# Stores of made left sides and pair outputs on GpSimd's queue, in an attention block followed by two wide layers

## The chip, the core and the metric

One core of a Trainium2 chip runs the whole program. Its engines work side by side, each through its own list of instructions in order: PE (TensorE, matrix products), ACT (ScalarE), DVE (VectorE), POOL (GpSimd) and SP (SyncE, which here only issues transfers between the device's memory, DRAM, and the core's memory, SBUF). A transfer (DMA) is issued by an engine's queue and then runs on the core's 16 DMA engines. The metric is the device time of one execution in microseconds (us); smaller is better.

## What is computed

An attention over pooled keys and values, then two layers with two matrix products each, on 4608 rows of 512 numbers, all in fp32 (the products' operands are split into a high and a low part, so each product is three matmuls).

```python
B, H, S, D = q.shape                      # 8, 8, 576, 64
k_p = k.reshape(B, H, S // 8, 8, D).mean(axis=3)   # and v_p the same
attn = softmax(q @ k_p.T / sqrt(D))
x = (attn @ v_p) rearranged to (B * S, H * D)      # 4608 x 512
h = x @ w_in                                       # 512 x 2048
x = maximum(0.01 * h, h) @ w_out                   # 2048 x 512
h = x @ w2_in
return (h * clip(h + 3, 0, 6) / 6) @ w2_out
```

## The kernel before

The kernel first writes down its whole work as a list of tasks, each with its engine, a cost, its inputs and its outputs, and a planner then simulates the engines on these costs and emits each engine's instructions in the order that it found. A transfer is a task of an engine called "dma" in that list, whatever queue issues it (on_dma, L294). Semaphores are put in from what each instruction reads and writes. Transfers of one queue take eight semaphores in turn, so a transfer also waits for the one eight before it on its queue to land.

The rows are cut in tiles of 512. The first three tiles go through the first layer as plain products (moe_tile), the rest in pairs of tiles (Pair1, in three pairs), and the second layer in five pairs of 920 or 924 columns (Pair). In a pair, a product of 2 x 2 blocks is computed with seven products (PRODUCTS, L863) of sums of blocks. Each of the seven needs a left side, a combination of weight blocks that is the same for every pair. Left sides are made once, while other products run, and kept in DRAM: first_weights (L925), pair_weights (L943) and second_weights (L975) load raw weights, decode them, combine quarters (combine, L911) and call split_off (L890). split_off takes one of three staging buffers called st, lets ACT cast the high part into it and DVE subtract to get the low part, and then issues two stores of 256 KB from it to DRAM (L906): one into the array for a pair's first product, one into that for its second. In second_weights the raw words come by a load of 1 MB (L982, raw<-wq), and ACT (L622, L624) and DVE (L627, L635) decode them.

A pair then streams left sides back from DRAM (stream, L1044; the load is L1049) into buffers that PE reads, in first (L1113) for its first product and second (L1219) for its second. second ends four times with a copy or sum of the result into an st buffer and a store of it (L1275): into x2 in DRAM for Pair1, into the output for Pair. Pairs also prepare the next pair's right sides from x2 (loads L1067).

All of these transfers, loads and stores alike, are issued by SP (DMA, that is nc.sync) in the planner's order. SP works strictly in order: a store whose data DVE has not yet made holds back the loads behind it, and a load whose buffer PE still reads holds back the stores behind it. GpSimd (GP, that is nc.gpsimd) only clears some buffers in the first 96 us.

Of the kernel before, what the change touches and what calls it, by code (L numbers as in the profile page):

```python
# [247 lines left out]
def attention_moe_moe(ctx: ExitStack, tc: tile.TileContext, qt, kt, vm, vr, wt, wq, eye, mask, out):  # L248
# [14 lines left out]
    PE, ACT, DVE, GP, DMA = nc.tensor, nc.scalar, nc.vector, nc.gpsimd, nc.sync  # L263
# [6 lines left out]
    def f32(ap):  # L270
        return ap.bitcast(F32)
# [22 lines left out]
    def on_dma(nbytes, emit, reads, writes):  # L294
        add("dma", nbytes / 340 + 60, emit, reads, writes)
# [4 lines left out]
    def copy(dst, src, n, psum=False, scale=None, extra=0):  # L300

        if scale is None:
            a = lambda: ACT.copy(out=dst.ap(), in_=src.ap())  # L303
            b = lambda: DVE.tensor_copy(out=dst.ap(), in_=src.ap())
        else:
            a = lambda: ACT.mul(out=dst.ap(), in_=src.ap(), mul=scale)  # L306
            b = lambda: DVE.tensor_scalar_mul(dst.ap(), src.ap(), scale)
        add("act", act_cost(n, psum) + extra, a, [src], [dst], other("dve", dve_cost(n, not psum), b))

    def subtract(dst, a, b, n):  # L310
        on_dve(
            n,
            lambda: DVE.tensor_tensor(out=dst.ap(), in0=a.ap(), in1=f32(b.ap()), op=ALU.subtract),  # L313
            [a, b],
            [dst],
        )
# [65 lines left out]
    def part(v, key, cut):  # L382
        return View(v.buf, (*v.key, key), lambda t: cut(v.cut(t) if v.cut else t))
# [503 lines left out]
    def new_st(dtype=F32):  # L887
        return buf("st", [128, 2, 512], dtype, 3)

    def split_off(left, f, v, s):  # L890

        st = new_st(F32R)
        src = View(v.buf, v.key, lambda t: v.cut(t).rearrange("p (g n) -> p g n", g=2))
        hi, lo = [st(i, lambda t, i=i: t[:, :, 256 * i : 256 * i + 256]) for i in range(2)]
        copy(hi, src, 512)
        subtract(lo, src, hi, 512)
        for g, (dst, cut) in enumerate(
            [
                (left.first[f // 2], lambda t: t[:, s, f % 2, :]),
                (left.second[s][f // 4], lambda t: t[:, f % 4, :]),  # L900
            ]
        ):
            dst = dst((s, f), cut)
            on_dma(
                262144,
                lambda dst=dst, g=g: DMA.dma_start(out=f32(dst.ap()), in_=f32(st.get()[:, g, :])),  # L906
                [st()],
                [dst],
            )

    def combine(left, f, q):  # L911
        (q11, q12), (q21, q22) = q
        plus(q22, q21, q22, 512)
        split_off(left, f, q22, 4)
        minus(q21, q11, q21, 512)
        split_off(left, f, q21, 3)
        minus(q11, q22, q11, 512)
        split_off(left, f, q11, 2)
        minus(q12, q12, q11, 512)
        split_off(left, f, q12, 6)  # L920
# [102 lines left out]
    class Pair:  # L1023
# [195 lines left out]
        def second(self, last=False):  # L1219

            n = self.n
            x, z, w = [[self.bank(k) for _ in range(2)] for k in "xzw"]
            y = {}
            for s in range(PRODUCTS):
# [3 lines left out]
                for f in range(8):  # L1228
# [10 lines left out]
                    b = [[self.slot(f, i, j) for j in range(2)] for i in range(2)]  # L1239
# [28 lines left out]
                if done:  # L1268
                    c, i, j = done
                    dst = self.place_of(i, j)  # L1270
                    for a, b in ((0, 1), (1, 2)) if last and s == 6 else ((0, 2),):
                        to, writes = dst(a, b)
                        on_dma(
                            256 * n * 2 * (b - a),
                            lambda c=c, a=a, b=b, to=to: DMA.dma_start(out=to(), in_=y[c].get()[:, a:b, 0:n]),  # L1275
                            [part(c, r) for r in range(a, b)],
                            writes,
                        )
# [82 lines left out]
    for u in units[: C["n32"]]:  # L1361
        g = u.g
        a = a13 if g else a12
# [254 lines left out]
```

## Time and profile before

| | us |
|---|---|
| three runs | 1597.93, 1599.67, 1600.58 |
| their median | 1599.67 |
| the profiled execution | 1599.98 |
| its span, first to last instruction | 1598.2 |
| PE busy in it | 1579.4 |
| DVE, ACT, GpSimd busy | 1187.1, 999.8, 2.3 |
| granted TensorE clock, mean | 0.997 |

The profiled execution is one run of the program, recorded by the chip. Busy time counts an engine's instructions; on PE the ends of matmuls are modelled. Rows of the timeline give start, duration, engine, line of the kernel, operation, what is written and read (names without buffer numbers), how many instructions were merged, and in brackets the idle time of the engine before it with what ended it. SPq rows are issues of transfers. Rows of waits give who waited for whom: total us, times, longest. A row of the table of stretches gives the stretch, its length, the busy time of PE, of PE's weight loads, of DVE, ACT and GpSimd with the count of instructions, then the granted TensorE clock as a share of full speed (2.4 GHz), the mean busy share of the 16 DMA engines, and GB/s. A tile's view gives duration in ns as least, median and most.

### The profile page before, as it was taken

How to read it: one execution, taken by the hardware profiler on the slowest of the kernel's cores; microseconds unless marked ns; L12 is line 12 of the kernel's file. 1: busy time of each engine (PE TensorE's matmuls, PEld its weight loads, DVE VectorE, ACT ScalarE, POOL GpSimd, SP SyncE). 2: the span in 40 equal slices, each digit the busy share in tenths (PEclk: the TensorE clock that was granted, in tenths of full speed). 3: DMA queues.
4: the chain of work that ended last, by engine and by line, in shares of the span. 5: the costliest groups of instructions: out<-in, count | busy, mean ns of one | idle time of the engine just before them, and what ended most of it. 6: DMA issues, size and time to landing. Idle time of an engine off the chain costs nothing.

```text
span 1598.2 us, 23912 instructions
## 1 busy us (share of the span) xinstructions
PE 1579.4 (99%) x8285; PEld 1350.3 (84%) x8285; DVE 1187.1 (74%) x2150; ACT 999.8 (63%) x2469; POOL 2.3 (0%) x12
## 2 busy tenths in 40 slices
PE   9999999999999999999989999999999999999999
PEld 8888887788788887878878888888888888888888
DVE  7989778677979776885687569658755955885494
ACT  6978577677977577666655455546545645654454
POOL 0000000000000000000000000000000000000000
PEclk9999999999999999999999999999999999999999
DMA  8988687668896898779988657856775686676564
GB/s 293 326 310 291 229 271 247 226 209 274 278 322 201 283 314 300 235 241 320 336 288 293 214 208 249 274 209 222 256 236 206 228 281 211 224 247 224 210 237 151
DMA packets 129480, 406.39 MB, mean 254 GB/s; under 512 B 18640, under 2 KB 47440, under 8 KB 107600
## 3 DMA queue, kind: packets, MB, share of 16 engines
q1 hardware_dynamic: 129360, 404.87, 74.3%
q8 instruction: 66, 1.08, 0.3%
q14 instruction: 54, 0.44, 0.1%
HBM read 317.79 MB, written 87.03 MB: 253 GB/s over the span
## 4 chain that ended last, share of the span: by engine, by line
PE 86%; DVE 6%; DMA 4%; ACT 2%; issue 1%; SPq 0%; ACTq 0%; DVEq 0%
PE y L1012 35%; PE h L1012 21%; PE a L1012 12%; PE y L757 2%; PE y L759 2%; PE y L758 2%; PE h L708 2%; PE h L710 2%; PE h L709 2%; PE a L466 2%; PE a L586 2%; PE a L541 1%; DMA raw<-vr 1%; DMA w<-left 1%; DMA x<-x 1%
## 5 line engine op out<-in xcount | busy, mean ns | idle before, releaser
L879 DVE TENSOR_TENSOR w<-y,w 128x512 f32<-128x512 f32 (+2 forms) x108 | 70.9, 658 | 114.3 <-PE y L1012 112.7
L306 ACT ACTIVATE gh<-w 128x460 fp32r<-128x460 f32 (+1 forms) x140 | 82.4, 589 | 65.4 <-PE y L1012 30.6
L879 DVE TENSOR_TENSOR w<-w 128x460 f32<-128x460 f32 (+2 forms) x168 | 105.4, 648 | 3.8 <-ACT w L723 3.4
L1207 DVE SCALAR_TENSOR_TENSOR gl<-w,gh 128x460 fp32r<-128x460 f32 (+1 forms) x140 | 88.9, 635 | 22.3 <-ACT gh L306 21.9
L1012 PE MATMUL y<-w,xh 128*128 128x512 f32 (+2 forms) x444 | 104.6, 384 | 0.4 <-ACT w L723 0.4
L1012 PEld LDWEIGHTS y<-w,xh 128*128 128x128 f32 x444 | 82.5, 188 | 14.1 <-ACT w L723 0.8
L491 ACT ACTIVATE s<-a,mx 96x72 f32<-96x72 f32 x264 | 79.8, 325 | 22.4 <-DVE mx L485 22.4
L757 PE MATMUL y<-gh,w 128*128 128x512 f32 (+2 forms) x220 | 85.0, 387 | 1.1 <-DVE raw L819 0.9
L1178 ACT ACTIVATE gh<-w,three 128x460 f32<-128x460 f32 (+1 forms) x60 | 40.9, 682 | 70.4 <-DVE w L879 70.4
L303 ACT CAST gh<-w 128x512 fp32r<-128x512 f32 x96 | 59.5, 622 | 40.4 <-PE y L1012 22.8
L1012 PE MATMUL y<-w,raw 128*128 128x460 f32 (+1 forms) x384 | 84.4, 373 | 0.0
L708 PE MATMUL h<-xh,w 128*128 128x512 f32 (+2 forms) x220 | 81.8, 372 | 0.0
L758 PE MATMUL y<-gl,w 128*128 128x512 f32 (+2 forms) x220 | 80.5, 366 | 0.6 <-DVE gl L313 0.6
L710 PE MATMUL h<-xh,w 128*128 128x512 f32 (+2 forms) x220 | 80.7, 367 | 0.3 <-DVE w L313 0.2
L759 PE MATMUL y<-gh,w 128*128 128x512 f32 (+2 forms) x220 | 80.6, 366 | 0.0
L709 PE MATMUL h<-xl,w 128*128 128x512 f32 (+2 forms) x220 | 80.4, 365 | 0.0
L313 DVE TENSOR_TENSOR gl<-w,gh 128x512 fp32r<-128x512 f32 x96 | 65.8, 687 | 19.2 <-ACT gh L303 18.7
L1012 PEld LDWEIGHTS y<-w,raw 128*128 128x128 f32 x384 | 72.4, 188 | 8.7
L1012 PE MATMUL y<-w,xl 128*128 128x512 f32 (+2 forms) x324 | 76.7, 385 | 0.0
L313 DVE TENSOR_TENSOR st<-raw,st 128x512 fp32r<-128x512 f32 x88 | 59.8, 685 | 14.4 <-ACT st L303 12.3
L1012 PE MATMUL y<-gh,raw 128*128 128x462 f32 (+1 forms) x224 | 69.4, 371 | 0.0
L1012 PEld LDWEIGHTS y<-w,xl 128*128 128x128 f32 x324 | 60.4, 188 | 10.4
(261 smaller groups left out, 4255.5 us busy)
## 6 DMA issues: line engine op xcount, KB each, us to landing
raw<-left SPq DMA_DIRECT2D x68, 1024.0 KB, 4.9
left<-st SPq DMA_DIRECT2D x176, 256.0 KB, 4.7
xh<-left SPq DMA_DIRECT2D x37, 1024.0 KB, 4.8
xl<-left SPq DMA_DIRECT2D x68, 512.0 KB, 4.8
xh<-left SPq DMA_DIRECT2D x56, 512.0 KB, 5.3
w<-left SPq DMA_DIRECT2D x56, 512.0 KB, 5.3
xl<-left SPq DMA_DIRECT2D x25, 1024.0 KB, 4.9
w<-wt SPq DMA_DIRECT2D x16, 1024.0 KB, 7.5
```

What stands on the lines that cost most here:

```text
L306: a = lambda: ACT.mul(out=dst.ap(), in_=src.ap(), mul=scale)
L313: lambda: DVE.tensor_tensor(out=dst.ap(), in0=a.ap(), in1=f32(b.ap()), op=ALU.subtract),
L491: ACT.activation(out=at()[:, c, h, :], in_=s4()[:, c, pi, :], func=AF.Exp, scale=1.0 / 64.0, bias=mx.get()[:, c, h : h + 1], accum_out=sm. ...
L708: PE.matmul(out=o, lhsT=hi, rhs=xh.get()[:, k, c0:c1], start=k == 0, stop=False)
L709: PE.matmul(out=o, lhsT=hi, rhs=xl.get()[:, k, c0:c1], start=False, stop=False)
L710: PE.matmul(out=o, lhsT=lo, rhs=xh.get()[:, k, c0:c1], start=False, stop=k == 3)
L757: PE.matmul(out=y[:, n0:n1], lhsT=hi, rhs=gh.get()[:, n0:n1], start=start, stop=False)
L758: PE.matmul(out=y[:, c0:c1], lhsT=hi, rhs=gl.get()[:, c0:c1], start=False, stop=False)
L759: PE.matmul(out=y[:, c0:c1], lhsT=lo, rhs=gh.get()[:, c0:c1], start=False, stop=stop)
L879: on_dve(n, lambda: DVE.tensor_tensor(out=dst.ap(), in0=a.ap(), in1=b.ap(), op=op), [a, b], [dst])
L1012: PE.matmul(out=o, lhsT=l, rhs=r, start=first and i == m == 0, stop=last and i == len(left) - 1 and m == 2, skip_group_check=True,)
L1207: lambda: DVE.scalar_tensor_tensor(out=lo.ap(), in0=v.ap(), scalar=1.0 / 6.0, in1=f32(hi.ap()), op0=ALU.mult, op1=ALU.subtract),
```

## The change

Two lambdas issue their transfer from another queue. The stores of left sides in split_off go from SP to GpSimd, all 176 of them. The stores of a pair's outputs in second go to GpSimd too, 28 of them, except in the last pair, whose five stay on SP. Everything else is as it was; loads stay on SP, as do other stores. The planner's task list, its costs and with them the order on PE, ACT and DVE are the same.

```diff
@@ split_off
             on_dma(
                 262144,
-                lambda dst=dst, g=g: DMA.dma_start(out=f32(dst.ap()), in_=f32(st.get()[:, g, :])),
+                lambda dst=dst, g=g: GP.dma_start(out=f32(dst.ap()), in_=f32(st.get()[:, g, :])),
                 [st()],
                 [dst],
             )
@@ Pair.second
                         on_dma(
                             256 * n * 2 * (b - a),
-                            lambda c=c, a=a, b=b, to=to: DMA.dma_start(out=to(), in_=y[c].get()[:, a:b, 0:n]),
+                            lambda c=c, a=a, b=b, to=to: (DMA if last else GP).dma_start(out=to(), in_=y[c].get()[:, a:b, 0:n]),
                             [part(c, r) for r in range(a, b)],
                             writes,
                         )
```

The order on SP near 600 us (st_N is a staging buffer, left1 and left2 the left sides of the two layers in DRAM, raw, xh, xl and w15 buffers in SBUF, wq the second layer's weights); a minus stands before rows that the queue no longer has:

```order
 L1049 DMA w15_6_4612<-left1_13_1_2137 128x1024
 L982 DMA raw_58_7065<-wq 128x2048
 L1049 DMA xh_5_4398<-left1_13_1_2137 128x1024 x2
-L906 DMA left2_260_1_3431<-st_101_6901 128x512
-L906 DMA left2_12_1_7140<-st_106_7080 128x512
-L906 DMA left2_201_1_7146<-st_106_7080 128x512
 L1049 DMA xl_5_4434<-left1_13_1_2137 128x1024
-L906 DMA left2_12_1_7140<-st_108_7144 128x512
 L319 DMA q_29_7186<-qt 128x576
-L906 DMA left2_251_1_7200<-st_108_7144 128x512
 L1049 DMA xl_5_4434<-left1_13_1_2137 128x1024
```

The stores between the loads are gone, the loads follow each other as before.

The order on SP near 790 us:

```order
 L1049 DMA xh_5_4398<-left1_13_1_2137 128x1024
-L906 DMA left2_13_1_8588<-st_137_8659 128x512
-L906 DMA left2_231_1_7386<-st_137_8659 128x512
-L906 DMA left2_13_1_8588<-st_138_8673 128x512
 L982 DMA raw_66_8724<-wq 128x2048
-L906 DMA left2_221_1_7356<-st_138_8673 128x512
 L1049 DMA xh_5_4398<-left1_13_1_2137 128x1024
 L1049 DMA xl_5_4434<-left1_200_1_1540 128x1024 x2
 L982 DMA raw_68_8791<-wq 128x2048
-L906 DMA left2_13_1_8588<-st_139_8685 128x512
-L906 DMA left2_261_1_7493<-st_139_8685 128x512
 L1049 DMA w15_6_4612<-left1_201_1_1977 128x1024 x2
```

Three stores ahead of raw_66 and two between raw_68 and the load into w15 have left the queue. The same place on GpSimd's queue, where nothing stood:

```order
+L906 DMA left2_13_1_8588<-st_137_8659 128x512
+L906 DMA left2_231_1_7386<-st_137_8659 128x512
+L906 DMA left2_13_1_8588<-st_138_8673 128x512
+L906 DMA left2_221_1_7356<-st_138_8673 128x512
+L906 DMA left2_13_1_8588<-st_139_8685 128x512
+L906 DMA left2_261_1_7493<-st_139_8685 128x512
```

They follow each other there with no load between them.

## Rows read from the trace of the kernel before

**Rows 1.** The page: busy us by engine, and a DMA issue's size and landing.
```profile
PE 1579.4 (99%) x8285; PEld 1350.3 (84%) x8285; DVE 1187.1 (74%) x2150; ACT 999.8 (63%) x2469; POOL 2.3 (0%) x12
...
left<-st SPq DMA_DIRECT2D x176, 256.0 KB, 4.7
```

**Rows 2.** Table of stretches.
```profile
118.00:880.00 762.00, 753.17 (x3924) 612.70 (x3925) 596.10 (x1087) 532.77 (x1489) 0.00 (x0) 1.00 0.81 271
880.00:1560.00 680.00, 679.29 (x3234) 607.24 (x3233) 472.07 (x821) 361.14 (x636) 0.00 (x0) 1.00 0.67 231
...
810.20:814.20 4.00, 3.99 (x11) 3.14 (x12) 3.97 (x7) 3.30 (x7) 0.00 (x0) 0.57 0.36 144
...
817.60:828.80 11.20, 11.14 (x48) 8.65 (x47) 11.20 (x19) 4.78 (x9) 0.00 (x0) 1.00 0.90 274
...
831.00:835.00 4.00, 4.00 (x11) 3.20 (x12) 3.17 (x6) 1.43 (x3) 0.00 (x0) 0.60 0.90 353
```

**Rows 3.** Timeline of PE: the four longest gaps between 600 and 840 us.
```profile
624.43 1.66 PE L1012 MATMUL y<-w,xh 128*128 128x512 f32 x6 [0.39 <-ACT w L723]
...
630.71 0.45 PE L559 MATMUL a<-ident,rem 96*96 96x96 f32 x3 [1.34 <-DVE tl L313]
...
810.21 0.67 PE L1012 MATMUL h<-gh,w 128*128 128x512 f32 x1 [2.11 <-DMA w<-left]
...
830.99 0.79 PE L1012 MATMUL h<-gh,w 128*128 128x512 f32 x1 [2.25 <-ACT st L303]
```

**Rows 4.** Waits on SP's queue, 118 to 890 us: total us, times, longest.
```profile
SPq L1049 <- PE y L1012: 161.6, 83, 5.1
...
SPq L906 <- DVE st L313: 77.7, 42, 6.9
```

**Rows 5.** Tile left: issue in ns; who waited for its transfers (us, times).
```profile
L906 SPq DMA_DIRECT2D left<-st x176: 319/423/1946, 118.5 to 849.3; - x176
...
  ACT st L303: 7.8, 7
...
  DVE st L313: 1.7, 1
```

**Rows 6.** Timeline of SP, ACT and DVE, 609 to 617 us.
```profile
609.53 1.44 SPq L906 DMA_DIRECT2D left<-st  x3
...
615.93 0.62 ACT L303 CAST st<-raw 128x512 fp32r<-128x512 f32 x1 [1.98 <-DMA left<-st]
...
616.58 0.69 DVE L313 TENSOR_TENSOR st<-raw,st 128x512 fp32r<-128x512 f32 x1 [1.67 <-DMA xl<-left]
```

**Rows 7.** Timeline of SP, 784 to 800 us.
```profile
784.33 0.39 SPq L1049 DMA_DIRECT2D xh<-left  x1
786.53 1.33 SPq L906 DMA_DIRECT2D left<-st  x3
787.91 0.93 SPq L982 DMA_DIRECT2D raw<-wq  x1
...
798.58 0.33 SPq L982 DMA_DIRECT2D raw<-wq  x1
799.01 0.86 SPq L906 DMA_DIRECT2D left<-st  x2
799.92 0.88 SPq L1049 DMA_DIRECT2D w<-left  x1
```

**Rows 8.** Timeline of ACT and DVE, 796 to 816 us.
```profile
796.22 0.67 ACT L622 ACTIVATE raw<-raw 128x512 f32<-128x512 f32 x1 [0.88 <-DMA raw<-wq]
...
808.82 0.69 DVE L627 SCALAR_TENSOR_TENSOR st<-raw,st 128x512 int32<-128x512 int32 x1 [2.73 <-ACT st L624]
...
815.54 0.69 DVE L313 TENSOR_TENSOR gl<-w,gh 128x512 fp32r<-128x512 f32 x1 [0.49 <-ACT gh L303]
```

**Rows 9.** DVE's copies by shape, 118 to 1560 us; GpSimd's last instruction.
```profile
L826 DVE COPY raw<-y 128x512 f32<-128x512 f32 x2 | 1.4, 692 | 2.0 <-PE y L759 1.9
...
95.58 0.28 POOL L744 MEMSET gh<- 128x224 f32 x1 [93.07 <-PE y L759]
```

## The prediction

> **What bounds the kernel now.** I read the page first: in its busy line PE (TensorE) stands at 1579.4 of a span of 1598.2 us [rows 1]. So nothing that the change touches can give back more than PE's idle time and the time in which PE ran at a lower clock. The table of stretches says where that is: 762.00 - 753.17 = 8.8 us of idle PE between 118 and 880 us, but only 0.7 us between 880 and 1560 us [rows 2]. The first stretch is where the left sides are made and stored, and where the other stores begin; the stores of the second layer's outputs lie in the other, which has nothing to give.
>
> PE's timeline then names the gaps worth having: 0.39 and 1.34 us near 624 and 631 us, 2.11 us at 810 us, 2.25 us at 831 us [rows 3]. Each of the last two is followed by 4 us at a granted clock of 0.57 and 0.60 of the 2.4 GHz level [rows 2], which costs 4.00 x 0.43 = 1.7 and 4.00 x 0.40 = 1.6 us more. All four with their clock are worth 1.73 + 3.8 + 3.9 = 9.4 us, 0.6% of the run. That is the ceiling of the change, apart from crumbs.
>
> Next, who holds up whom on SyncE's queue (SP). In 118 to 890 us the loads of left sides (L1049) wait 161.6 us there for one kind of PE instruction alone, since their buffers are still being read; stores of left sides (L906) wait 77.7 us for DVE's subtraction [rows 4]. The queue is in order: each of these waits also holds everything behind it, a store behind a load that has no buffer, and a load behind a store that has no data.
>
> **What the change does to the queues.** 176 stores of left sides and 28 of pair outputs leave SP for GpSimd, which had nothing left to do after its last memset; the last pair's five output stores stay. PE, ACT and DVE keep their order to the row. On SP the loads keep their order among themselves. SP loses 176 issues at a median of 0.42 us [rows 5], about 75 us spread over 730 us of a queue that mostly waits: by itself that is worth nothing on the path.
>
> **Term 1, a store that came late (600 to 635 us).** The staging tile st has three buffers, so ACT's cast into the next one waits until both stores of the one three before have landed. At 609.53 us SP issues three stores at once, the first of them the second store of st_101, which had stood behind loads of left sides; ACT then sits idle 1.98 us until a store has landed, and DVE 1.67 us for the same ring [rows 6]. The chain of waits goes on from there through DVE and ACT to PE's gap of 1.34 us at 631 us. On GpSimd no load stands ahead, the store leaves before 609 us, and the two waits should go. If both PE gaps go with them, the gain is 0.39 + 1.34 = 1.73 us; if something else is late at the same place it is 0. What could be late next is the attention unit's exponentials in the same chain. I take the whole 1.7, since PE's two gaps together are no longer than DVE's or ACT's wait alone.
>
> **Term 2, loads behind stores (783 to 836 us).** At 786.53 us three stores leave SP, one after the other as DVE finishes them, and behind the last stands the load of raw_66 (weights of the second layer), issued at 787.91 us. The load in front of them left at 784.33 us and took 0.39 us, so without them raw_66 could leave up to 787.91 - 784.72 = 3.2 us earlier [rows 7]. But its reader is ACT, in order behind other work, and was held only 0.88 us by that landing [rows 8]. The decode can therefore end at most 0.88 us earlier, and the next load of the kind, raw_68, which waits for this decode, leaves at 797.70 instead of 798.58 us. Behind it stood two more stores and then the load of w, at 799.92 us [rows 7]; without the stores it goes at 797.70 + 0.4 = 798.1 us, 1.8 us earlier and with two stores of 256 KB less ahead of it [rows 1]. PE waited 2.11 us for that very load [rows 3], so this gap shrinks to 0.3 us or nothing.
>
> That gain is not kept, for DVE is late next. DVE was idle 2.73 us until raw_68 had landed and been read by ACT, and from 808.82 us on it works almost without a break, with one wait of 0.49 us at 815.54 us [rows 8] and all of 817.6 to 828.8 us busy [rows 2], up to what PE waits for at 830.99 us [rows 3]. So PE's restart at 831 us moves only as far as DVE's start does: 0.88 us if raw_68 lands earlier by that alone, 2.73 + 0.49 = 3.2 us if it lands so early that DVE never waits. I take 1.8 us, the middle, because raw_68 shares the DMA engines with its neighbours whichever queue issues them. The gap at 831 us then grows by about what the gap at 810 us loses.
>
> **Term 3, what GpSimd's issuing costs.** The trace before shows no DMA issued by GpSimd, so I bound it. One issue on SP took 319 to 1946 ns [rows 5]; the only thing GpSimd does in the trace late on is a memset of 0.28 us [rows 9]. I take the middle of SP's own range, 1.1 us, which puts the second store of a tile 2 x 1.1 - (0.32 + 0.42) = 1.5 us later wherever SP issued at once. Where it hurts is the ring again: the waits for these stores were 7.8 us in 7 waits on ACT's casts and 1.7 us in one on DVE, 9.5 us in 8 [rows 5]. About half of these are held stores, which get better; say the other four and as many that were just in time grow by 1.5 us each, 12 us on ACT and DVE. Of the 9.5 us PE felt 1.7 us (term 1); at that share, 0.18, the growth costs PE 2.2 us. The cover is ACT's idle 229 us and DVE's 166 us in this stretch [rows 2]. Ends: 0 (issues as fast as SP's, all hidden) and 12 x 0.54 = 6.5 us, if ACT's delay reaches PE three times as often. I take 1.0 us, nearer the low end, because the held stores, which start up to many microseconds earlier, take some of these waits away.
>
> The Trainium skill, "DMA: Bandwidth & Descriptors", in its table of specifications, gives a first-byte latency of about 1 us on GpSimd's path and 0.6 us on SyncE's; by that difference alone, an estimate, the second store of a tile would be some 0.4 us later and term 3 near 0.3 us. No row here shows it.
>
> **The sum.** -1.7 - 1.8 + 1.0 = -2.5 us on the profiled execution's 1599.98 us gives 1597.5; the median of the three runs, 1599.67, lies 0.3 us lower, so 1597.2 us. The two-tenths of a per cent that a measurement of this kernel can tell from no change are 3.2 us: the lines are 1596.5 and 1602.9 us. My sum falls just inside.
>
> **The rivals.**
> All late work moves up together. For it: between 720 and 880 us stores go out as soon as DVE is done, DMA engines never run empty for want of an issue, and then both big gaps and their low clock go: 1599.67 - 9.4 + 0.5 = about 1591 us. Against it: DVE has no idle time from 817.6 to 828.8 us to give [rows 2].
>
> Nothing moves. The loads that PE needs wait for PE's own buffers (L1049 in [rows 4]) and for bandwidth, and the held stores were early enough nearly everywhere. Then the gaps stay: 1599.7 us, give or take 1. The Trainium skill, "DMA: Bandwidth & Descriptors", under "Issuing engines are not separate DMA queues", speaks for this: all issuing engines share the 16 DMA engines, and a second one saves only the sequencer's issue time, usually small. By that rule alone this rival would be the result. What speaks against it in the rows is that the issue order here holds other transfers back, for whole microseconds.
>
> Slower: the ring of three. If a store from GpSimd lands two or more microseconds later than one from SP where SP was free, ACT waits at most reuses, and the in-order casts behind it feed PE. A PE gap of 2.1 us cost 3.8 us with its clock. One or two such gaps, without term 1 and with term 2 at its low end of 0.9, make 1599.67 + 3.8 - 0.9 = 1602.6 to 1606.4 us; I put it at 1604.5. It decides once issue and landing of a tile's two stores take over 2 us more than SP's. The Trainium skill, "SBUF — State Buffer", under "Who interferes with whom", gives a reason: DVE copies, casts and scalar operations in their two-port modes lock GpSimd out of a shared port. DVE's copies and casts in this stretch are six instructions, the longest two 0.69 us each [rows 9], so by that rule nothing is added here.
>
> That the change does not take effect is excluded: the order of instructions shows the 204 issues on GpSimd.
>
> **How the numbers follow.** The forecast, 1594.5 to 1599.5 us, has 0.42, of which 0.20 lie below 1596.5 us. All late work moves up: 0.18. Nothing moves: 0.19. Slower: 0.21, of which 0.01 stays inside the line. So faster 0.20 + 0.18 = 0.38, same 0.22 + 0.19 + 0.01 = 0.42, slower 0.20. The range runs from 1590.5 us (just past the first rival) to 1604 us: it leaves out about 0.05 below and half of the slower case above, some 0.15 in all.
>
> **What would show it.** Right: no idle of ACT before 616 us for a landed store; the load of w near 798 us issued within 1 us after raw_68's; PE's gap at 810 us under 0.5 us with no low clock behind it, and the one near 831 us still there, at 2 us or more. The first rival: neither gap, no stretch of low clock after 118 us. Nothing moves: the same four gaps. Slower: waits of ACT and DVE for left stores above 9.5 us in total, new PE gaps before 350 us, where stores were never held up. I am wrong at the root if GpSimd's issues take over 2 us each, or if PE's gaps appear where no store is near.

## The result, and the profile after

The changed kernel took 1620.8 us (median of 4 runs, 1616.25 to 1625.72) beside 1599.95 us for the kernel before on the same chip: a ratio of 1.0133, 95% interval 1.0111 to 1.0155. It is slower by 21 us; the forecast was 1597.2 us, the range ended at 1604. The profiled execution of after, 1616.25 us, was its shortest, so its trace shows 16.3 of the 21 us; the two longest have a mean granted clock of 0.995, the other two 0.998.

The page of before, for the one queue that it uses (packets, MB, share of 16 engines):
```profile
q1 hardware_dynamic: 129360, 404.87, 74.3%
```
The page of after: busy us by engine; the queues; the costliest GpSimd group (busy, mean ns, idle before); landing of the left stores.
```profile
PE 1583.7 (98%) x8285; PEld 1348.6 (84%) x8285; DVE 1186.7 (74%) x2150; ACT 997.8 (62%) x2469; POOL 115.1 (7%) x216
...
q1 hardware_dynamic: 97936, 344.88, 62.6%
q0 software_dynamic: 17600, 59.99, 9.7%
...
L906 POOL DMA_DIRECT2D left<-st x176 | 94.9, 543 | 476.0 <-DVE st L313 317.5
...
left<-st POOLq DMA_DIRECT2D x176, 256.0 KB, 5.5
```
Against [rows 1], PE's busy time grew by only 4.3 us while its span grew by 16.3: 12 us are new idle time. The stores land 5.5 us after their issue instead of 4.7, and GpSimd is busy 0.54 us with each issue.

The table of stretches of after, cut at the same places of the work as the first two lines of [rows 2] (the last column but two is PE's granted clock):
```profile
118.50:892.50 774.00, 756.24 (x3901) 611.84 (x3901) 594.69 (x1085) 530.17 (x1486) 99.75 (x186) 1.00 0.78 267
892.50:1575.50 683.00, 680.55 (x3231) 606.67 (x3230) 471.97 (x821) 360.74 (x635) 12.55 (x18) 1.00 0.66 230
```
In the first stretch PE is idle 17.8 us instead of 8.8; in the second, which I had written off as having nothing to give, 2.5 instead of 0.7.

PE's gaps in after (start, us, engine, line; in brackets the idle time before and what ended it):
```profile
125.97 0.50 PE L758 MATMUL y<-gl,w 128*128 128x512 f32 x1 [1.56 <-DVE gl L313]
...
176.69 0.56 PE L466 MATMUL a<-keys,q 64*96 64x72 f32 x7 [2.76 <-ACT tr L303]
...
640.77 0.45 PE L559 MATMUL a<-ident,rem 96*96 96x96 f32 x3 [0.56 <-DVE tl L313]
...
806.84 3.07 PE L1012 MATMUL y<-w,w 128*128 128x512 f32 x12 [1.96 <-ACT w L303]
...
842.27 0.51 PE L1012 MATMUL h<-gh,w 128*128 128x512 f32 x1 [2.84 <-ACT st L303]
```
Of the four gaps in [rows 3], the one of 0.39 us is gone, 1.34 became 0.56, the one of 2.11 us at 810 us is gone with its low clock, and 2.25 became 2.84: in this trace that is the pattern that terms 1 and 2 named. But there are new ones: at 126 and 177 us, where the kernel before had 0.25 us and none, and at 807 us. Matmul by matmul, PE starts 0.8 us earlier than before at 42 us, 3.9 us later at 177 us, 9.5 at 300, 11.4 at 560, 12.5 at 890 and 16.0 at the end.

Who waited for the stores in after (tile left: issue in ns as least/median/most, then us and times), to be read against [rows 5]:
```profile
L906 POOL DMA_DIRECT2D left<-st x176: 540/540/687, 118.0 to 861.2; - x176
...
  ACT st L303: 19.7, 15
  ACT st L624: 8.0, 5
  DVE st L304: 1.2, 1
```
These three are the waits of the ring of three: 28.9 us in 21, where the prediction said that 9.5 us would be the mark of the slower case.

### The profile page after: what moved, and what is told of

Its sections match the earlier page's. It is cut to its first block, busy times and chain, and to the rows that moved or that the text cites. A ratio compares the mean times of both kernels' runs of the same rounds, so it can differ in the third digit from the quotient of the medians.

```text
span 1614.5 us, 23978 instructions
## 1 busy us (share of the span) xinstructions
PE 1583.7 (98%) x8285; PEld 1348.6 (84%) x8285; DVE 1186.7 (74%) x2150; ACT 997.8 (62%) x2469; POOL 115.1 (7%) x216
## 3 DMA queue, kind: packets, MB, share of 16 engines
q1 hardware_dynamic: 97936, 344.88, 62.6%
q0 software_dynamic: 17600, 59.99, 9.7%
## 4 chain that ended last, share of the span: by engine, by line
PE 65%; DVE 11%; DMA 11%; issue 6%; ACT 5%; SPq 1%; POOL 1%; ACTq 0%; DVEq 0%; POOLq 0%
PE y L1012 27%; PE h L1012 18%; PE a L1012 10%; DMA left<-st 3%; DMA x<-x 3%; PE y L757 1%; DMA raw<-wq 1%; PE y L759 1%; PE y L758 1%; DMA raw<-vr 1%; DVE st L313 1%; ACT s L491 1%; PE a L586 1%; DVE w L313 1%; PE a L466 1%
## 5 line engine op out<-in xcount | busy, mean ns | idle before, releaser
L906 POOL DMA_DIRECT2D left<-st x176 | 94.9, 543 | 476.0 <-DVE st L313 317.5
L303 ACT CAST st<-raw 128x512 fp32r<-128x512 f32 x87 | 54.1, 629 | 34.5 <-DMA left<-st 19.1
```

The lines of the kernel that those rows point to most:

```text
L906: lambda dst=dst, g=g: GP.dma_start(out=f32(dst.ap()), in_=f32(st.get()[:, g, :])),
```

## The experiments

All ratios are to the kernel before on the same chip; L906 is the line of the left stores, L1275 that of the outputs.

### Which stores cost: parts add up

```diff
 L906  - DMA.dma_start(            + GP.dma_start(                              (e1: left stores only)
 L1275 - DMA.dma_start(            + (DMA if last else GP).dma_start(           (e2: outputs only)
 L906  - DMA.dma_start(            + (GP if left is left2 else DMA).dma_start(  (e3: second layer only)
```
e1. 

> Only the 176 stores of left sides (L906) go out from GpSimd; all pair outputs stay on SyncE. Ring theory (GpSimd's stores of a tile land later where SyncE was free, ACT and DVE wait in the ring of three, PE gets gaps): nearly the whole loss is here, PE's start at 880 us of before comes 11 to 12 us later as with the whole change, the waits of ACT and DVE for left stores are near 29 us, and the time is 1611 to 1617 us. Order theory (the loss is that outputs no longer stand behind the loads of x on one queue): about 1600 us, with PE on time until 889 us. Sharing theory (two queues that run at the same time slow every transfer): 1611 to 1617 us as well, but with loads that take longer from issue to landing than before.

Measured: 1614.9 us, ratio 1.0102 (1.0080 to 1.0124). The time fits the ring theory and the sharing theory alike. The median way of loads from issue to landing, 118 to 905 us, moved both ways (keys from kt 5.3 to 6.2 us, w from left 5.3 to 4.9), so it does not choose between them.

e2. 

> Only the 28 stores of pair outputs (L1275, the last pair's left out) go out from GpSimd; the stores of left sides stay on SyncE. Order theory: PE loses 3 to 5 us after 889 us, at the restarts near 1000, 1283 and 1424 us, where the loads of x for the next pair land 5 us later: 1603 to 1605 us. Ring theory alone: no difference, 1599 to 1601 us, waits in the ring as before (12 us).

Measured: 1603.9 us, ratio 1.0038 (1.0023 to 1.0052), as the order theory said; in its trace PE falls back by 3.4 us after 890 us.

e3. 

> Only the stores of the second layer's left sides (112 of the 176, none before about 200 us) go out from GpSimd. Ring theory: the gaps at 125, 177 and 196 us (some 6 to 7 us of PE's delay) go, the held stores after 600 us still gain as in the whole change (3 to 4 us), the delays between 220 and 560 us stay (4 to 5 us): 1599 to 1604 us. Sharing theory: the loss goes by the number of stores moved, 112/204 of 21 us, 1609 to 1613 us.

Measured: 1606.5 us, ratio 1.0049 (1.0032 to 1.0067): between the two expectations.

Left stores and outputs both cost, and 1.0102 + 0.0038 is about the whole of 1.0133. Later two runs split the left stores by time:
```diff
 L906  - DMA.dma_start(   + (GP if int(st.name[3:]) < 95 else DMA).dma_start(    (e21: made before 560 us)
 L906  - DMA.dma_start(   + (GP if int(st.name[3:]) >= 95 else DMA).dma_start(   (e22: made after 560 us)
```
e21. 

> Three buffers of st; only the 106 left stores made before 560 us (st 5 to 85) go out from GpSimd. If the parts of the loss add up and lie where the traces of the whole change put them: ratio 1.008 to 1.011, 1611 to 1616 us, nearly the whole loss of the left stores (1.0102). If the loss is spread by the number of stores: 106/176 of it, 1.006, about 1608 us.

Measured: 1611.6 us, ratio 1.0078 (1.0062 to 1.0093).

e22. 

> Three buffers of st; only the 70 left stores made after 560 us (st 95 and up) go out from GpSimd: terms 1 and 2 of the prediction with their own share of term 3. By the prediction's terms 1 and 2: 3.5 us less than before, ratio 0.998, with no gap near 631 and 810 us and the one near 831 us kept. By what the traces of the changed kernel show there (new gap at 807 us after ring waits, gap at 810 us gone): within 1.5 us of before, ratio 0.999 to 1.001. If the four buffers made the gain of the run with late stores (0.9976), this one has none or a loss.

Measured: 1603.8 us, ratio 1.0022 (1.0008 to 1.0036). So 106 early stores cost 0.78%, 70 late ones 0.22%, 28 outputs 0.38%. The late ones, which by terms 1 and 2 should have gained, cost as well.

### After 560 us: the ring of three

In e22 ACT waits for left stores 20.7 us after 570 us, and PE has a gap that is not in [rows 3]. ACT's waits (us, times, longest), then PE's timeline:
```profile
ACT st L303 <- DMA left<-st: 19.4, 12, 3.4
...
ACT st L624 <- DMA left<-st: 1.3, 1, 1.3
```
```profile
630.88 0.45 PE L559 MATMUL a<-ident,rem 96*96 96x96 f32 x3 [1.31 <-DVE tl L313]
...
798.23 4.38 PE L1012 MATMUL y<-w,w 128*128 128x512 f32 x12 [2.81 <-ACT w L303]
```
The wait of 3.4 us ends at 793.95 us, and the cast of w that PE needs at 798 us stands behind it in ACT's order. The gap near 631 us is as long as before (1.34 us): ACT's wait of 1.98 us at 616 us is gone, but one cast later it waits 1.30 us for another left store. The gap near 810 us is gone, the one near 831 us is 3.54 us. To test the ring, st got a fourth buffer where it is allocated, with the order on every engine kept:
```diff
-            self.tile = pool.tile(shape, dtype, name=self.name, tag=tag, bufs=bufs)
+            self.tile = pool.tile(shape, dtype, name=self.name, tag=tag, bufs=bufs + (tag == "st"))
```
With it, three more edits: late left stores on GpSimd, and of the outputs only each pair's last three (e20); nothing else, the control (e10); the whole change (e9).
```diff
 L906  + (GP if int(st.name[3:]) >= 95 else DMA).dma_start(                      (e20)
 L1275 + (DMA if last or c == "c11" else GP).dma_start(                          (e20)
```
e20. 

> Four buffers of st, left stores on SyncE until 560 us and on GpSimd after that (st 95 and up), the last three outputs of each pair on GpSimd, the first on SyncE. If the change gains where only stores and loads of left sides meet (the traces of the runs with the change come 3 to 4 us nearer to the kernel before between 577 and 877 us) and loses only before 560 us and at the first outputs: 1591 to 1595 us. If the gain at 810 us is given back at 831 and 877 us: 1595 to 1599 us.

Measured: 1593.9 us, ratio 0.9976 (0.9965 to 0.9986). ACT's waits for left stores after 570 us, and two rows of PE's timeline (from 785 to 830 us the second is the only gap of over 0.25 us):
```profile
ACT st L303 <- DMA left<-st: 2.1, 2, 1.6
```
```profile
629.52 0.45 PE L559 MATMUL a<-ident,rem 96*96 96x96 f32 x3 [0.94 <-DVE tl L313]
...
825.34 0.50 PE L1012 MATMUL h<-gh,w 128*128 128x512 f32 x1 [2.08 <-ACT st L303]
```
Ring waits 21.3 us (with 0.6 us of DVE) to 2.1, the gap near 798 us gone, the one near 810 us gone too, the one near 831 us still there, but with no low clock behind it (1.00 in the 4 us after it, 0.60 before). Matmul by matmul PE gains 3.9 us at the gap near 810 us, which is its 2.11 us and their low clock, and keeps them to the end: with a ring long enough the stores do what term 2 said at that place, and more is kept than it said. Of term 1 nothing comes: with no ring wait left there, 0.94 of the 1.34 us near 631 us stay, and between 560 and 700 us PE gains 0.1 us. e20 differs from e22 in the outputs too; these alone gave no measurable gain (e8, below), though in e8's trace, too, the gap near 810 us is shorter (1.32 us).

e10. 

> The kernel before with four buffers of st, the order on every engine kept: the control for the run beside it. Ring theory: the kernel before waited only 12 us in the ring, of which PE felt about 2 us: 1595 to 1599 us. If a fourth buffer is worth as much here as in the changed kernel, the ring has nothing to do with GpSimd.

Measured: 1596.1 us, ratio 0.9987 (0.9973 to 1.0001): the fourth buffer is worth little where SyncE stores, less than the 0.46% that lie between e22 and e20. The gap near 810 us stays, so it was not the ring that held PE there:
```profile
811.56 0.67 PE L1012 MATMUL h<-gh,w 128*128 128x512 f32 x1 [2.40 <-DMA w<-left]
```
Over all traces this gap is 0.44 to 2.40 us in the seven where all late left stores leave from SyncE (shortest in e21 and e2, where other delays bring PE late to it), and at most 0.19 us in the thirteen where both stores of a late tile, its second store or the held ones leave from GpSimd. But in time the intervals of e10 and e20 overlap: that e20 is faster than the fourth buffer alone is read from the trace, and the runs do not show it.

e9. 

> The whole change, with four buffers of the staging tile st in place of three and the order on every engine kept. Ring theory: the waits of ACT and DVE for left stores fall from 29 us to a few us, the gaps at 126, 177, 226, 301 and 455 us go, and of the loss of 21 us only the outputs' 6 us stays: 1600 to 1606 us. If the stores on GpSimd cost through something else (slower loads beside them, the burst of other stores on SyncE at 119 us), the time stays above 1612 us.

Measured: 1612.9 us, ratio 1.0078 (1.0056 to 1.0101). The ring waits fell from 28.9 to 7.0 us, as the ring theory asks, but more than half of the loss stayed. The ring is not the whole cause.

### Before 560 us: loads that lost their place

```diff
 L906  + (GP if int(st.name[3:]) < 95 else DMA).dma_start(     (e23: e21 with the fourth buffer)
```
e23. 

> As the run with the early left stores alone on GpSimd (ratio 1.0078), with four buffers of st. Ring theory for the early stretch: the fourth buffer takes the loss away as it did after 560 us, ratio 0.998 to 1.001. Order theory (the loads of the attention units land later because stores run beside them, whatever the ring): most of the loss stays, ratio 1.004 to 1.008, ACT's and DVE's waits for left stores before 560 us are under 7 us and DVE's waits for raw from kt, vm and vr over 20 us.

Measured: 1605.9 us, ratio 1.0053 (1.0040 to 1.0066), as the order theory said: of e21's 0.78%, 0.25% is gone (0.13% of it is what the fourth buffer gives the kernel before, e10), and two thirds stay. The waits that a DMA ended, 118 to 570 us in before and 118 to 582 us (the same work) in e23:
```profile
DVE raw L372 <- DMA raw<-vm: 9.6, 4, 4.7
DVE raw L372 <- DMA raw<-vr: 4.0, 3, 1.5
...
DVE raw L819 <- DMA raw<-yp: 1.9, 1, 1.9
DVE raw L879 <- DMA raw<-chunk: 1.6, 1, 1.6
ACT st L624 <- DMA left<-st: 1.3, 1, 1.3
...
ACT st L303 <- DMA left<-st: 0.5, 2, 0.3
```
```profile
DVE raw L372 <- DMA raw<-vm: 13.6, 4, 5.5
DVE keys L372 <- DMA raw<-kt: 5.6, 2, 3.5
ACT st L624 <- DMA left<-st: 4.5, 2, 3.8
DVE raw L372 <- DMA raw<-vr: 3.5, 3, 1.9
...
DVE raw L879 <- DMA raw<-chunk: 2.5, 2, 2.1
DVE raw L819 <- DMA raw<-yp: 2.2, 1, 2.2
```
Ring waits are 1.8 us before and 4.5 in e23; DVE's waits for loads are 17.1 us before and 27.4 in e23. (With three buffers, e21, it is 15.0 and 24.8; in the whole change 13.5 and 24.1.) The fourth buffer takes away most of the ring waits, and DVE's waits for loads stay. One load shows why: keys for an attention unit (raw from kt, KB, us from issue to landing), before and in e23:
```profile
raw<-kt SPq DMA_DIRECT2D x1, 576.0 KB, 5.5
```
```profile
raw<-kt SPq DMA_DIRECT2D x1, 576.0 KB, 8.4
left<-st POOLq DMA_DIRECT2D x2, 256.0 KB, 7.8
```
Before, the load left SyncE at 206.43 us, and three left stores at 206.81 to 207.78 us, behind it; the load was served first. In e23 the two stores left GpSimd at 213.04 and 213.57 us, the load SyncE at 213.84 us, and all three were under way together. DVE waited 3.5 us for those keys, for which it did not wait before.

Three runs try this by itself, on the load of raw from vm near 184 us and the four tiles whose stores surround it, and on the held stores (HELD lists the tiles whose first, g = 0, or second, g = 1, store had been held):
```diff
 L906  + (GP if 29 <= int(st.name[3:]) <= 32 else DMA).dma_start(     (e19: on the kernel before)
 L906  + (DMA if 29 <= int(st.name[3:]) <= 32 else GP).dma_start(     (e18: on e9)
 L906  + (GP if int(st.name[3:]) in HELD[g] else DMA).dma_start(      (e17: on the kernel before)
```
e19. 

> The kernel before with only these eight stores (st 29 to 32) on GpSimd, everything else on SyncE. Order theory: the load of raw from vm at 184 us lands in 6 us or more instead of 4.4 us, DVE waits 5 to 6 us for it instead of 3.4 us, PE gets gaps of 1.5 to 3.5 us between 193 and 222 us that it did not have, and the time is 1.5 to 4 us above the kernel before, 1599 to 1602 us. If these eight do no harm: within 1 us of the kernel before, and the loss of this stretch comes from tiles further ahead.

Measured: 1599.8 us, ratio 1.0007 (0.9996 to 1.0017). The load, with its neighbours, 182 to 187 us, before and in e19:
```profile
left<-st SPq DMA_DIRECT2D x6, 256.0 KB, 6.1
raw<-vm SPq DMA_DIRECT2D x1, 512.0 KB, 4.4
```
```profile
left<-st POOLq DMA_DIRECT2D x6, 256.0 KB, 6.7
raw<-vm SPq DMA_DIRECT2D x1, 512.0 KB, 6.3
```
The load lands 1.9 us later, DVE waits for it 5.4 us instead of 3.4, and PE is 1.8 us later at 196 us in the trace. For this load the mechanism is shown; its effect on the whole time (1.6 us of medians) is too small to be told from none. The profiled execution was the longest of the 13 (1607.6 us): PE loses 5.7 us more behind 230 us, where nothing differs from the kernel before. A single trace can stray by that much, and small shifts of PE between traces are to be read with that in mind.

e18. 

> The whole change with four buffers of st (1612.9 us), and only the eight stores of the four left tiles that are made between 177 and 187 us (st 29 to 32), beside the load of raw from vm, back on SyncE. Order theory (that load is served first where the stores stand behind it on one queue): the load lands 4.4 to 5 us after its issue instead of 6.8 us, DVE's wait for it falls from 5.85 to under 4 us, the gaps of PE between 195 and 201 us go, PE's start at 230 us comes 2 to 3.5 us earlier against the kernel before than with all of them on GpSimd (7.7 us), and the time is 1609.5 to 1611 us. Start theory (each store on GpSimd costs by its own later landing in the ring): under 1 us of change, 1612 to 1614 us.

Measured: 1612.2 us, ratio 1.0082 (1.0062 to 1.0102), no better than e9. The load landed in 5.4 us instead of 6.8 and DVE waited 4.4 instead of 5.8 us, so the order worked on the load; but PE's delay at 228 us was 6.5 us against 7.7, a gain below the expected 2 to 3.5 us, and the time did not follow: it lies where the start theory put it.

e17. 

> Only the 43 left stores that SyncE issued more than 2.3 us after their data were there in the kernel before (15 tiles with both stores, 13 with the second) go out from GpSimd; the rest and all outputs stay on SyncE. This is terms 1 and 2 of the prediction without term 3. If those terms are right: -2 to -4 us, 1595 to 1598 us, with the gap near 810 us under 0.5 us. If the held stores cost nothing where they were: 1599 to 1600 us.

Measured: 1603.3 us, ratio 1.0028 (1.0013 to 1.0042). This run moves just the stores that SyncE had held, and it is slower, with 8.2 us of ring waits, no more than before. The gap near 810 us is gone, but PE gets gaps of 0.93 and 0.62 us at 195 and 224 us and one of 2.45 instead of 0.95 us at 271 us, and waits for loads grew (raw from chunk 1.6 to 3.3 us, from yp 1.9 to 2.7, from wq 9.5 to 15.2). One of the held stores left GpSimd at 183.05 us, ahead of the load of raw from vm at 183.72 us, which landed in 6.1 us instead of 4.4. Here the hold had protected the load.

e13 tried to give the order back the other way, on e9, by sending the attention units' loads from GpSimd too:
```diff
 L319 - lambda: DMA.dma_start(   + lambda q=GP if len(plan.tasks) > 700 else DMA: q.dma_start(
```
e13. 

> The whole change with four buffers of st (1612.9 us), and from about 121 us on the attention units' loads (L319: keys, values, queries) also go out from GpSimd, so that these loads and the left stores stand on one queue again, in the order of the kernel before. Order theory (loads of the attention units lost their place ahead of the stores and share the DMA engines with them): DVE's waits for raw from kt, vm and vr fall from 25.1 us to 16 to 18 us as before, the gaps of PE between 174 and 230 us mostly go, and the time is 1606 to 1609 us. If the order of these loads against the stores has no part in it: 1612 to 1614 us; if GpSimd's path makes a load as late as it makes a store: above 1614 us.

Measured: 1618.8 us, ratio 1.0140 (1.0115 to 1.0164). Worse, and in the range of the third case; but raw from vm landed 6.0 us after its issue (6.2 in e9), so the loads were not slower on that queue. DVE's waits for raw from kt, vm and vr stayed at 23.3 us, where the order theory wanted 16 to 18. On one queue again, these loads also stand behind stores that wait for DVE, and stores behind loads of q that wait for PE (130.8 us in 18 waits of GpSimd, 118 to 590 us). It neither supports nor refutes the order theory, since it brought waits of its own.

### The outputs: the same, at four places

Each pair's first output store leaves about 1 us behind the two loads of x that ACT needs next. Waits for these loads, 985 to 1440 us, in before and then in e2:
```profile
ACT w L303 <- DMA x<-x: 10.5, 4, 3.7
DVE x L879 <- DMA x<-x: 7.8, 4, 3.1
```
```profile
ACT w L303 <- DMA x<-x: 14.2, 4, 4.0
DVE x L879 <- DMA x<-x: 11.7, 4, 3.4
```
At one of them, before, SyncE issues the loads and then the store; in e2 GpSimd's store leaves beside the second load:
```profile
1273.11 1.18 SPq L1067 DMA_DIRECT2D x<-x  x2
1274.39 1.11 SPq L1275 DMA_DIRECT2D out<-st  x1
```
```profile
1272.93 0.60 SPq L1067 DMA_DIRECT2D x<-x  x1
```
```profile
1273.01 0.72 POOL L1275 DMA_DIRECT2D out<-st  x1 [100.37 <-DVE st L879]
```
The second load landed 8.0 us after its issue before, 9.8 in e2. It is later at three of the four places; near 1131 us it is not (9.5 and 8.9 us).
```diff
 L1275 - DMA.dma_start(   + (DMA if last or c == "c11" else GP).dma_start(     (e8: first output back)
```
e8. 

> Left stores on SyncE, and of each pair's four output stores the last three on GpSimd, the first (c11, issued about 1 us behind two loads of x on SyncE's queue) back on SyncE. Order theory (on one queue the loads of x are served before that store, on two they share the DMA engines with it): the loss of 6 us of the run with all outputs on GpSimd goes, ACT's waits for x from 990 us on go back from 3.2 to 4.0 us at each of the four boundaries to 2.0 to 3.7 us, and the time is 1597 to 1600 us. If it is GpSimd's path in general that costs, the three stores left there keep three quarters of the loss: 1602 to 1604 us.

Measured: 1598.2 us, ratio 0.9988 (0.9974 to 1.0001), with ACT's waits for x at 10.4 us as before. All of the outputs' loss came from seven stores, the first of each pair; the other 21 cost nothing that can be measured. Four of the seven are those that no longer stand behind the loads of x; what the other three, of the first layer's pairs, ran beside was not looked at. The outputs use the ring of st too: ACT waits 2.2 us for output stores in e2 and 2.1 us in e8, and not at all before.

### How late a store on GpSimd is

```diff
 L906  + (GP if g else DMA).dma_start(                                           (e5; e12: with the fourth buffer)
 L906  + (g or GP.tensor_copy(out=late.get(), in_=f32(st.get()[:, 0, 0:256])), GP.dma_start(...))   (e14: on e1)
```
e5. 

> Of the two stores of each left tile only the second goes out from GpSimd (88 issues), the first stays on SyncE. If the start is what counts (0.41 us from DVE's end to GpSimd's first issue and 0.54 us more to the second, against 0.03 and 0.4 us on SyncE), the second store starts as early as it did before, the ring waits fall to below 18 us and the time to 1600 to 1605 us. If the landing is what counts (5.5 us from GpSimd's issue against 4.7 us), the second store is as late as in the whole change and the time is near 1610 to 1615 us.

Measured: 1601.5 us, ratio 1.0016 (1.0006 to 1.0027), with ring waits of 7.9 us on ACT. Landing of the left stores in e5:
```profile
left<-st POOLq DMA_DIRECT2D x88, 256.0 KB, 5.0
left<-st SPq DMA_DIRECT2D x87, 256.0 KB, 4.2
```
Here g is 0 for a tile's first store and 1 for its second. One store from GpSimd lands 5.0 us after its issue, not 5.5. A tile is then complete about as early as before; only two on GpSimd in a row are late.

e14. 

> Only the left stores on GpSimd (1614.9 us, 31.98 us of ring waits on ACT), and ahead of the first store of each tile GpSimd also copies 128x256 elements of the tile, which starts both stores later by the length of that copy (to be read from the profile; taken as 0.5 us here). If the start of the stores sets the loss, ACT's ring waits grow by more than 10 us and the time by 4 to 9 us, 1619 to 1624 us. If the loss comes from sharing the DMA engines, not from the start: 1613 to 1617 us.

Measured: 1630.8 us, ratio 1.0208 (1.0188 to 1.0228). The copies took 1.05 us on average (0.81 median, 8.86 the longest), many of them beside DVE's subtraction; over the 88 tiles the first issue came 1.22 us after the data on average instead of 0.71 in e1, and the ring waits of ACT rose from 32.0 to 42.3 us. Half a microsecond went with 1%, more than the 4 to 9 us expected. The dose is not pure: DVE's busy time rose by 7.4 us beside GpSimd's copies.

e12. 

> The second store of each left tile on GpSimd, the first and all outputs on SyncE, and four buffers of st. If a ring long enough leaves only the gain (stores that no longer stand behind loads, loads that no longer stand behind stores): 1590 to 1596 us. If the two queues' sharing costs something by itself: 1598 to 1602 us, as with three buffers.

Measured: 1596.3 us, ratio 0.9981 (0.9970 to 0.9991), not clear of the fourth buffer alone (e10, 0.9987); in its trace, too, PE gains 3.9 us at the gap near 810 us. e16 added e8's outputs to e12:

e16. 

> Four buffers of st, the second store of each left tile on GpSimd, and each pair's last three output stores on GpSimd, the first on SyncE. If the three small gains add (0.9981 for the second store with four buffers, 0.9988 for the outputs): a ratio near 0.997, 1593 to 1596 us. If the gains are the same idle time counted twice: 1595 to 1598 us.

Measured: 1597.5 us, ratio 1.0006 (0.9995 to 1.0017). The gains do not add, and e12's 0.9981 does not come back; I have no explanation for that. e20 and e12 lie below the kernel before by more than their intervals, but e16 shows that a gain of this size, a quarter of a per cent, does not hold from one such version to the next.

## Why the prediction was wrong

**The step that failed is term 3**, +1.0 us (6.5 at most) where the change as a whole lost 21. It failed in three places. The rival "slower" named the signs that came, ring waits far above 9.5 us and new gaps before 350 us, but its price of one or two gaps, 1606.4 us at most, missed as well.

First, its count. I let half of the eight waits of [rows 5] and as many that were just in time grow by 1.5 us each, 12 us in all. (The 1.7 us on DVE among them ends, by its row in [rows 6], with a load of left sides; the cast that DVE needs had ended 0.03 us before it starts, so this is ACT's wait counted a second time.) A store that never made anyone wait does not show in a table of waits, and there were many with little to spare: in the trace of before, about 40 of the 88 tiles landed less than 1.5 us before the next use of their buffer began. The waits for left stores went from 9.1 us (7.8 of them on ACT's casts, in [rows 5]) to 28.9, those before 560 us from 1.8 to 13.5. What I needed was the time from each tile's landing to the next use of its buffer.

Second, its size per store was nearly right, for other reasons. The issue took 0.54 us, not 1.1, but GpSimd starts late. The start after DVE's subtraction, in before (SyncE) and in after (GpSimd):
```profile
137.58 0.69 DVE L313 TENSOR_TENSOR st<-raw,st 128x512 fp32r<-128x512 f32 x1
...
138.29 2.60 SPq L906 DMA_DIRECT2D left<-st  x4
```
```profile
140.01 0.69 DVE L313 TENSOR_TENSOR st<-raw,st 128x512 fp32r<-128x512 f32 x1
...
141.10 0.54 POOL L906 DMA_DIRECT2D left<-st  x1 [14.39 <-DVE st L313]
```
0.02 us after the end of the subtraction on SyncE, 0.40 us on GpSimd. From the data of a tile to the landing of its second store, the median over the 39 tiles made before 320 us went from 4.88 to 6.29 us. Tile by tile, the 20 of them that SyncE had issued at once landed 1.3 us later (median), where I had said 1.5; only 0.5 of it is the later start of the second store, the rest a longer way from issue to landing. The 10 that SyncE had held landed 1.9 us earlier. The rival "ring of three" was a right mechanism with the wrong point of decision: 1.3 us was enough, not over 2. It is not the whole cause: with a fourth buffer 7.0 us of ring waits and 0.78% of loss remain (e9).

Third, and missing from every term and rival: **the order of one queue also protects**. I counted what SyncE's order held back as something to gain. e17 moves just that and loses 0.28%; e2 and e8 show a loss from seven output stores alone. In the cases that I followed (e19, e17, e23, e2) a store behind a load let the load through first, and on two queues the load landed 1.7 to 2.9 us later.

**Term 2** was right about the gap near 810 us: in after the load of w leaves 0.43 us behind that of raw (811.41 and 810.98 us) and the gap is gone. That only 1.8 us of it would be kept behind 831 us was wrong where the ring was long enough: in the traces of e12 and e20 all 3.9 us are. In after and in e22 a new gap of 1.96 and 2.81 us, from the ring, stands just ahead and takes them back. **Term 1** was too large: in after 0.39 + 0.78 us of the two gaps went, but with the late stores on GpSimd the longer one stays at 1.34 us in e1 and 1.31 in e22, and with no ring wait at that place (e20) at 0.94. So only part of it hung on the ring. Between 560 and 700 us PE gains 2.0 us in after, but 0.1 in e20, and loses 1.1 and 1.4 in e1 and e22. (My comparison was off as well: 1.73 us is more than DVE's wait of 1.67.)

"Nothing to give" for the second layer's outputs was true and not the question: a stretch without idle time can still lose, 3.4 us in e2's trace after 890 us.

The Trainium skill's section that I weighed ("DMA: Bandwidth & Descriptors", "Issuing engines are not separate DMA queues") would have had no change; it says that a second engine saves only issue time, and is silent on what it costs. The same page, under "Queues, rings and completion order", says that each DMA engine takes turns between the queues that have work. The load of 512 KB that took 4.4 us with the stores behind it and 6.3 us with them on another queue agrees with that; I had not drawn the consequence. That DVE would not lock GpSimd out, as I had taken from the Trainium skill, "SBUF — State Buffer", under "Who interferes with whom", the trace bears out: the issues of left stores take 540 to 687 ns each, and DVE's busy time is 1187.1 us before and 1186.7 after. My count there was short, though: the rule names scalar operations too, and DVE has at least 72 short ones in that stretch (158 and 165 ns on average).

What stays open: how the loss before 560 us divides. A third at most went with the fourth buffer (e21 to e23). That the rest is the loads' lost place fits DVE's waits for them (17.1 to 27.4 us) and single loads (e19), but e18, which gave one load its place back, won 1.2 us in the trace and nothing in time. That the rest is many such places of 1 to 2 us is argued, not shown: I did not undo them one by one. Nor does a run separate the second queue as such from GpSimd's: with the queue, the size of the packets changed too (the last section), and no run sends the stores from a third engine.

## What to carry to other kernels

Before a store is moved to another queue, list what stands behind and ahead of it: a load that was ahead was being served first, and will share from now on. A later landing costs through a ring whose waits are still zero, so measure the slack of each buffer, not the waits. Move only the stores that overtake no load that an engine waits for, and lengthen the ring with the move (e20: 0.9976, with a fourth buffer, the stores of the first 560 us and each pair's first output left where they were; the fourth buffer alone, e10, gave 0.9987, and the two are not clear of each other).

## What the hardware showed that I had not expected

GpSimd's issue of a left store is nearly constant, 540 ns (median) to 687, and keeps it busy; its start lies 0.40 us behind the instruction that releases it, against 0.02 us on SyncE (medians over all tiles 0.41 and 0.03). The path itself is not slower by much once alone: 5.0 us from issue to landing for a tile's second store in e5, against 4.9 for the second from SyncE in before (4.2 for the first from SyncE in e5).

The same stores come in other packets. GpSimd's queue moves 59.99 MB in 17600 packets, 3.4 KB each; SyncE's queue has 129360 - 97936 = 31424 packets fewer for these bytes, 1.9 KB each. Most are of 4 KB and 2 KB, and take 0.16 and 0.08 us of a DMA engine.

A small copy on GpSimd (128x256, 1.05 us mean) is slow and reaches beyond GpSimd. Its rows in e14, and DVE's subtraction into st beside it (busy us, mean ns):
```profile
L906 POOL COPY late<-st 128x256 f32<-128x256 f32 x88 | 92.8, 1054 | 566.5 <-ACT st L303 565.0 <-DVE st L304 1.4
```
```profile
L313 DVE TENSOR_TENSOR st<-raw,st 128x512 fp32r<-128x512 f32 x88 | 62.4, 715 | 35.6 <-ACT st L303 35.4
```
The subtraction took 715 ns on average instead of 685 without these copies.
